# A spectral filter and an MLP on one core: a new order of loads, transposes and matmuls

## The chip, the cores and the metric

The kernel runs on one core of one Trainium2 chip. The metric is the device time of one execution in microseconds. The kernel before took 152.96 us, the median of three runs (152.87 to 153.53). The profiled execution took 152.75 us; the span from its first to its last instruction, which the profile's pages count from, is 151.0 us.

## The reference

The input x has 2048 tokens of 640 features (bf16). Each token is normalized, and the normalized xn goes two ways. One is a filter in the frequency domain over tokens and features together; the other is a two-layer MLP. Both results and the input are added.

```python
xn = _layernorm(x, axis=-1)
X  = rfft2(xn.astype(float32)) * (w_r + 1j * w_i)        # 2048 x 321 frequencies
A  = irfft2(X).astype(bfloat16)
h  = gelu(xn @ w1 + b1)                                  # 640 -> 1536, tanh form
out = x + A + (h @ w2 + b2)                              # 1536 -> 640
```

## The kernel before

**Tiles.** The 2048 tokens lie on 128 partitions, 16 to each; tile c holds token c of every partition. A tile is 128 by 640.

**Normalization.** For each tile VectorE takes statistics in two halves (`bn_stats`, L584), joins them (L588), adds epsilon (L596), GpSimd takes the power -1/2 for two tiles at a time (L597), and VectorE normalizes (L617). The result, xn, goes two ways.

**MLP.** The first layer needs xn with the features on the partitions, `xnT`. A tile is transposed either by TensorE (five transposes into PSUM at L635, then copied out by VectorE or ScalarE) or by a DMA transpose that SyncE issues (L624); the list `BYDMA` says which tiles go by DMA. The first layer then runs over six blocks of tiles (`BLOCKS`: one, one, two, four, four, four tiles, so matmuls of 128, 256 and 512 columns) and over twelve slices `fc` of 128 of W1's 1536 columns; each slice of a block is five matmuls into one PSUM bank, which ScalarE turns into `gT` by gelu with the bias b1 (L688). W1 is loaded in three parts by `W1P`: slices 0 to 2 on ScalarE's queue, slices 3 to 6 and 7 to 11 on SyncE's. The second layer takes `gT` against W2 (four loads) and accumulates a tile's 640 outputs in two banks (`second`).

**Filter.** The Fourier transforms are matmuls with constant tables. Pairs of tiles are folded on VectorE (L650 and L654, into `xf`), multiplied by table G into `XV` (PSUM tile `aps`, eight of them), transformed along the features with table E (`bps`, groups b0 to b5 given by `GROUPS`), then along the short token axis with table M (`cps`, blocks c00 to c31 in the trace's name mtab), multiplied by the filter W on VectorE (L756, L760), and sent back by table N (`dps`, d00 to d31, ntab). These come out as `U`, are transposed by DMA (L781), go through table GE (`eps`, getab), are unfolded on VectorE (L806, L811), and the last table, H, adds them to the second layer's sums in PSUM (`fin`). VectorE adds x + b2, prepared at L834 (L865), and SyncE stores the tile. For tiles in `KEEP` the second layer's sum is made early and moved out of PSUM (L856), and the H product is added later. The filter's weights w_r and w_i come in 34 loads (`load_w`), all of which the first product at L756 waits for.

**What sets the order.** All instructions are first recorded as operations with estimated durations, priorities and dependences. A planner (`Sched.schedule`) then walks time forward and fixes one order for each engine: among what can start now it takes the highest priority. `PRIO` and `DELTA` shift priorities by kind and by buffer name, `HOLD` tells how long TensorE should look for work of the same tile shape before it changes shape, `CHAIN` fixes the order of the blocks b, c and d on TensorE, `ZONE` says in which of the eight PSUM banks each kind may stand, and late times (`WLATE` for filter weights, `W2LATE`, `HLATE`) hold a load back in the plan. A late time acts in the plan only: on the chip a queue issues its next load as soon as the waits of that load allow. SyncE's loads and transposes form one list, issued one after another; a transpose whose tile isn't normalized yet holds what stands behind it. TensorE begins with idle matmuls on zeros (`idle`, `WARM`), which stand before the first tile's transposes and between them and the first layer.

Of the kernel before, what the change touches and what calls it, by code (L numbers as in the profile page):

```python
# [13 lines left out]
D = 640  # L14
# [4 lines left out]
NFC = 12  # L19
# [68 lines left out]
HOLD = 0.08  # L88
DELTA = {'w1_1': -129.7, 'hps3_0': -215.2, 'hps5_11': -20.4, 'xe4': -26.5, 'hps3_1': -406.2, 'hps5_10': -17.0, 'hps3_3': -30.1, 'fps0_0': -223.7, 'fps7_0': -5.0, 'gT3_9': -7.7, 'hps2_11': -58.5, 'hps0_8': -390.4, 'w2_3': -67.4, 've': 53.7, 'xo4': -78.8, 'xf2': 1.3, 'gT2_8': -76.4, 'xo1': -127.1, 'cps0_1': -49.2, 'bps3': 15.1, 'e': -84.2, 'w2_1': -191.5, 'xnT14': -64.0, 'fps10_0': 12.5, 'xo2': 243.3, 'xnT15': 63.3, 'T7': 4.7, 'hps0_4': -4.8, 'st': -0.2, 'xnT6': -28.6, 'hps3_5': 72.7, 'T5': 6.2, 'hps0_0': -3.4, 'xnT5': 123.1, 'hps2_3': 3.6, 'hps2_2': -1.6, 'fps15_320': -4.3, 'yf4': 155.4, 'xf5': -104.0, 'gT5_1': -418.7, 'hps0_9': -56.7, 'xe5': 3.3, 'hps3_8': 5.3, 'U4': 12.0, 'fps6_0': 15.4, 'dps3_1': 192.6, 'mhalf': -22.4, 'xb5': 3.0, 'xb2': 82.5, 'xa5': -49.0, 'gT5_10': 6.4, 'xn2': 44.4, 'gT4_3': -9.0, 'T1': -6.3, 'aps4': -66.2, 'hps4_4': 50.5, 'xa3': -129.6, 'v15': 32.5, 'hps2_6': 67.9, 'xz6': 13.4, 'hps4_3': -8.7, 'xo10': -7.1, 'T3': -3.8, 'fps15_0': 6.4, 'cps2_1': -0.7, 'hps1_0': -49.1, 'gT0_11': -3.3, 'hps2_4': 22.7, 'os13': -338.9, 'hps5_9': -3.2, 'bps5': 28.3, 'v11': 122.4, 'gT0_2': -677.2, 'fps4_0': 10.3, 'gT0_9': -325.4, 'gT4_11': -102.1, 'gT5_3': -117.0, 'y21': 54.8, 'w2_0': 11.4, 'x12': -26.0, 'hps5_2': -12.3, 'xo8': -10.3, 'yo5': -2.7, 'Z3': 4.8, 'U7': -4.4, 'T0': 3.1, 'hps0_2': -54.0, 'gT2_4': -47.7, 'dps0_0': -63.5, 'hps0_7': -4.6, 'Z7': 118.6, 'gT0_1': -10.6, 'hps3_2': 7.1, 'os7': 9.5, 'gT3_11': -10.1, 'hps1_9': -20.0, 'Y4': -450.7, 'xnT2': 90.2, 'gT4_4': -5.7, 'yf2': 102.2, 'dps3_0': -32.1, 'xo14': 11.6, 'xa2': -0.3, 'xo9': 2.7, 'hps1_1': 170.0, 'yo0': -59.2, 'aps0': 2.3, 'eps5': 0.9, 'hps4_11': 318.5, 'xe6': -0.6, 'eps0': 22.7, 'v5': -23.8, 'xnT13': 4.1, 'gT1_7': 42.0, 'xa6': -90.2, 'U6': -8.9, 'xo7': 5.8, 'xb0': -1.4, 'T2': -49.8, 'os11': -257.0, 'gT2_9': 3.5, 'aps7': -113.2, 'U3': 10.3, 'hps5_7': -1.6, 'yo4': -12.5, 'gT0_4': -4.4, 'fps15_480': -17.1, 'xnT8': 8.7, 'm': -24.0, 'gT5_6': -0.1, 'xo15': 26.7, 'gT3_5': 540.8, 'v1': 6.6, 'hps4_10': 60.2, 'gT1_1': -33.1, 'fps1_0': 5.7, 'y22': -24.0, 'v13': -2.1, 'kps14': -347.4, 'gT0_5': -532.0, 'gT3_4': -9.8, 'gT3_1': 11.0, 'hps1_7': -10.2, 'gT4_8': -4.3, 'U2': -7.0, 'xf4': -31.0, 'gT1_11': 290.2, 'y20': -7.8, 'os10': 30.9, 'cps2_0': -344.1, 'xb3': 4.5, 'gT5_11': 123.8, 'os14': 8.4, 'os9': 65.8, 'hps1_11': 12.0, 'xf6': -24.4, 'hps3_11': -5.3, 'n': 5.9, 'fps3_0': 460.6, 'bps1': -6.0, 'gT5_0': -18.0, 'gT2_10': 3.2, 'gT4_2': 17.5, 'y25': -40.9, 'bps0': 128.4, 'hps2_9': 28.0, 'hps1_2': -0.5, 'i': -429.4, 'gT3_10': 15.1, 'hps1_3': -7.0, 'warmps': -3.7, 'hps2_8': 20.8, 'xn7': -55.7, 'gT2_7': -25.5, 'os5': 133.8, 'xo3': 12.3, 'bps2': 124.2, 'tps3': -7.1, 'os3': -90.6, 'xz4': 303.0, 'wpad': -63.1, 'v4': -13.7, 'v3': 57.5, 'b2': -2.7, 'b1ps': 451.6, 'xnT9': 7.8, 'fps2_0': -19.4, 'gT0_10': -130.4, 'hps4_7': 11.2, 'aps1': -23.2, 'x14': -2.7, 'gT3_8': 8.6, 'gT4_1': 259.1, 'kps10': -242.3, 'dps0_1': 0.6, 'gT1_4': 26.9, 'cps3_1': -20.9, 'gT1_8': 388.6, 'Y0': 3.7, 'xa1': -9.0, 'xnT7': 15.0, 'xnT0': -4.2, 'xz14': -15.5, 'x8': -20.9, 'gT5_8': 5.6, 'xe3': -0.6, 'dps1_0': 163.0}


def mm_us(n):
    return max(n / 2400.0 + 0.0027, 0.0265)
# [286 lines left out]
GROUPS = ((0, 2), (2, 3), (5, 3), (8, 3), (11, 3), (14, 2))  # L380
BYDMA = (4, 8, 9, 10, 11, 12, 13, 14, 15)
WLATE = (14.6, 0.72)
ANY = [(0, 8)]
ZONE = {'hps': [(4, 8)], 'bps': [(0, 4), (4, 8)], 'cps': [(0, 4)], 'dps': [(0, 4)], 'eps': [(0, 4)], 'fin': [(0, 8)], 'fps': [(4, 8)], 'tps': [(0, 8)], 'aps': [(0, 8)]}
PRIO = {'hps': -118.5, 'gelu': -251.6, 'pb': 89.9, 'pc': 206.3, 'filt': 461.0, 'ipc': 165.5, 'eps': 24.1, 'fin': -47.0}
AHEAD = 1
EARLY = 4
CHAIN = "b0 b1 c01 c00 b2 c10 d00 d01 c11 b4 b3 c21 c20 d10 d11 b5 c31 d21 d20 c30 d30 d31".split()
XASPLIT = [((0, 1, 2, 3, 4),)] * 7 + [((0, 1), (2, 3, 4))]
KEEP = (2, 3, 4, 5, 7, 8, 12)  # L390
RES = 261.9
W2LATE = (31.0, 2.4)
HLATE = 59.8
WARM = (46, 6)
X2POS = 2
FLAG = 1.4
# [3 lines left out]
def bass_parallel_sum__spectral_gfnet__dense_activation_gelu__prompt_kernel(  # L400
# [21 lines left out]
    with ExitStack() as es:  # L422
# [54 lines left out]
        def load(dst, src, buf, nbytes, after=(), reads=(), rate=395e3, q="sp", late=0.0):  # L477
            return K.op([(q, 0.6 if buf is B_w else 1.0 if q == "pool" else 0.45)], 20 if q == "pool" else 400, lambda e, _: e.dma_start(dst, src), reads=reads, writes=[buf], after=after, nbytes=nbytes, rate=rate, late=late)  # L478
# [35 lines left out]
        idle(WARM[0], 5.25 - 0.1 * (55 - WARM[0]))  # L514
# [61 lines left out]
        norm_ops, ring_ops, a_ops, first_ve = [], [], [], []  # L576
        B_rs = [Buf(f"rstd{c}") for c in range(16)]
        for c0, n in [(0, 1), (1, 1)] + [(c, 2) for c in range(2, 16, 2)]:
            pr = 100 - c0 / 2
            B_mv, B_ve, B_r = Buf("mv"), Buf("ve"), Buf("r")  # L580
            for c in range(c0, c0 + n):
                B_st = Buf("st")
                for h in range(2):
                    st = K.op([("dve", 0.393)], pr, lambda e, _, c=c, h=h: e.bn_stats(stats[:, c, 6 * h:6 * h + 6], view(X, c * D + H2 * h, [[1, H2]])),  # L584
                         reads=[B_x[c]], writes=[B_st], gate=first_ve if c == 1 else [])
                if c == 1:
                    second_st = st
                K.op([("dve", 0.119)], pr, lambda e, _, c=c: e.bn_aggr(mv[:, c, :], stats[:, c, :]), reads=[B_st], writes=[B_mv])  # L588
            a, b = c0, c0 + n
            if not c0:  # L590
                o = K.op([("act", 0.2)], 300, lambda e, _: e.activation(ve[:, 0:1], mv[:, 0, 1:2], ACT.Sqrt, bias=epst[:]), reads=[B_mv, B_eps], writes=[B_ve])
                K.op([("dve", 0.09)], 110, lambda e, _: e.reciprocal(rstd[:, 0:1], ve[:, 0:1]), reads=[B_ve], writes=[B_r])
                K.op([("act", 1.45)], 300, lambda e, _: e.activation(first[:, 1:2], warm[:, 0:1], ACT.Gelu_apprx_tanh), reads=[B_warm], gate=[o])
                first_ve = [o]
            else:
                K.op([("dve", 0.09)], pr, lambda e, _, a=a, b=b: e.tensor_scalar_add(ve[:, a:b], mv[:, a:b, 1], 1e-5), reads=[B_mv], writes=[B_ve])  # L596
                K.op([("pool", 0.65)], pr, lambda e, _, a=a, b=b: e.tensor_tensor(out=rstd[:, a:b], in0=ve[:, a:b], in1=mhalf[:, a:b], op=ALU.pow),  # L597
                     reads=[B_ve, B_mh], writes=[B_r])
            for c in range(a, b):
                B_rs[c].writers += B_r.writers + B_mv.writers  # L600

        for pair in range(8):
# [10 lines left out]
            for n in range(2):  # L613
# [9 lines left out]
                if c in BYDMA:  # L623
                    K.op([("sp", 1.3)], 500, lambda e, _, c=c, n=n, xnv=xnv: e.dma_start_transpose(xnT[:, :, 128 * c:128 * c + 128], xnv(n, 0, [[1, D]])),  # L624
# [12 lines left out]
                tp = K.op([("pe", 5 * mm_us(128))], pr, xt, reads=[B_xn, xn, B_id], writes=[tps], alts=[[("128", 5 * mm_us(128))]])  # L637
                if not c:
                    pe([("128", 0.1)], 200, lambda: [(psb(B_b1ps.slot, [[1, NFC]]), b1t[:], ident[0:NFC, 0:NFC], True, True)], reads=[B_b1, B_id], writes=[B_b1ps], gate=[tp])
                    K.op([("act", 0.2)], 200, lambda e, _: e.activation(b1col[:], psb(B_b1ps.slot, [[1, NFC]]), ACT.Copy), reads=[B_b1ps], writes=[B_b1c])  # L640
                    idle(WARM[1], WARM[1] * mm_us(128), gate=[tp])
                for k, (js, engs) in enumerate(EVAC[c] if c < 2 else [((0, 5), "both")]):
                    w = 128 * (js[1] - js[0])
                    K.op([x for x in (("dve", 0.066 + w / 1860.0), ("act", act_us(w))) if engs in ("both", x[0])], pr,
                         copy(lambda c=c, js=js: xnT[:, js[0]:js[1], 128 * c:128 * c + 128],
                              lambda tpv=tpv, js=js: tpv(*js).rearrange("p (j t) -> p j t", j=js[1] - js[0])),
                         reads=[tps], writes=[B_xnT[c]] + ([B_xnTp[c][k]] if c < 2 else []))
            pr = 100 - pair - FLAG
# [75 lines left out]
        for P in range(4):  # L724
# [53 lines left out]
            for pair, U, B_u in zip(two, Us, B_us):  # L778
                for qq in range(2):
                    q = 2 * pair + qq  # L780
                    K.op([("sp", 1.3)], 500, lambda e, _, q=q, qq=qq, U=U, uv=uv: e.dma_start_transpose(  # L781
# [12 lines left out]
        for gi, (c0, n) in enumerate(GROUPS):  # L794
# [20 lines left out]
            for i in range(n):  # L815
# [18 lines left out]
                res_ops.append(K.op([("dve", 0.74)], RES - c / 10, lambda e, _, c=c, xov=xov, shaped=shaped: e.tensor_tensor(  # L834
# [67 lines left out]
```

## Time and profile before

| what | value |
|---|---|
| time, median of 3 | 152.96 us |
| span of the profiled execution | 151.0 us |
| TensorE busy | 142.7 us, 95% |
| VectorE busy | 114.2 us, 76% |
| ScalarE busy | 81.0 us, 54% |
| the filter weights' issues on SyncE | 34, from 7.2 to 52.0 us |
| W1's parts: issue to landing | 480 KB 4.3 us, 800 KB 6.6 us, 640 KB 12.0 us |
| DMA transposes of xn: to landing | 2.7 / 3.0 / 4.6 us (least, median, most) |
| last store issued | 148.97 us |

A busy TensorE isn't TensorE at its peak: matmuls overlap[...]. The starts of matmuls that stand in a row tell the pace better: ten of 128 columns take 0.56 us, seven of 512 columns 1.51 us. The engines' starts in the timelines are counted from the first instruction. "SPq" is SyncE issuing a DMA; the time shown is that of the issue, and the landing comes later. A wait is put down to what released the instruction last, and "issue" means that the profile shows no releaser.

### The profile page before, as it was taken

Reading aid. Unit: us, or ns where it says so; the run is one execution under the profiler, and the core shown is the slowest. Engines: PE = TensorE matmul, PEld = TensorE weight load, DVE = VectorE, ACT = ScalarE, POOL = GpSimd, SP = SyncE. Lnnn points to the kernel's source line nnn. Section 1 sums busy time; section 2 is a strip of 40 time slices with the busy share of each in tenths; the row PEclk is TensorE's granted clock in tenths of the full one; section 3 lists DMA queues with packets and bytes.
Section 4 is the critical chain, followed back from the end, with each engine's and each line's share of the span. In section 5 each row is a group of like instructions: output and inputs, shape, how many; then the busy total and the mean of one; then the engine's idle time right before and its main releaser. Section 6 shows DMA issues by size and latency. Waiting matters only on the chain.

```text
span 151.0 us, 4055 instructions
## 1 busy us (share of the span) xinstructions
PE 142.7 (95%) x1701; PEld 88.3 (58%) x1725; DVE 114.2 (76%) x244; ACT 81.0 (54%) x143; POOL 9.3 (6%) x22
## 2 busy tenths in 40 slices
PE   7999899999999997999998999999999999999993
PEld 7879797544556352355354455555667665655573
DVE  1899998999932579497999999942489998656433
ACT  3679989765896779678999471230124204100000
POOL 1120341124000000000000000000000000000000
DMA  4999977668898575083006406215100232202022
GB/s 128 360 400 386 218 125 156 132 130 122 220 212 172 131 207 218 4 114 64 2 4 83 95 4 122 56 21 119 40 0 6 85 130 87 87 4 107 23 87 87
DMA packets 29609, 17.93 MB, mean 119 GB/s; under 512 B 18424, under 2 KB 28280, under 8 KB 29592
## 3 DMA queue, kind: packets, MB, share of 16 engines
q1 hardware_dynamic: 28552, 16.47, 42.9%
q0 software_dynamic: 240, 0.69, 2.3%
q10 hardware_dynamic: 800, 0.52, 1.1%
q8 instruction: 13, 0.21, 0.6%
q14 instruction: 4, 0.03, 0.1%
HBM read 10.96 MB, written 2.62 MB: 90 GB/s over the span
## 4 chain that ended last, share of the span: by engine, by line
PE 75%; DMA 8%; ACT 5%; DVE 4%; SPq 4%; issue 3%
PE ps L483 75%; DMA W<-in_B_w_dram 8%; SPq L478 4%; DVE T L756 2%; ACT gT L688 1%; DVE Z L760 1%; ACT T L496 1%; ACT U L496 1%; ACT XV L496 1%; DVE Y L497 1%; DVE xnT L856 0%; ACT Y L496 0%; ACT xnT L496 0%; DVE W L865 0%
## 5 line engine op out<-in xcount | busy, mean ns | idle before, releaser
L483 PE MATMUL ps<-xnT,W 128*128 128x512 bf16 (+2 forms) x350 | 55.0, 306 | 2.1 <-issue 1.0
L483 PE MATMUL ps<-W,gT 128*128 128x512 bf16 (+3 forms) x384 | 54.5, 293 | 1.3 <-issue 0.6
L483 PEld LDWEIGHTS ps<-W,gT 128*128 128x128 bf16 x396 | 30.1, 98 | 22.6 <-issue 1.2
L483 PEld LDWEIGHTS ps<-xnT,W 128*128 128x128 bf16 x360 | 28.7, 98 | 22.1 <-issue 2.1
L688 ACT ACTIVATE gT<-ps,b1col 128x512 bf16<-128x512 f32 (+2 forms) x72 | 36.4, 554 | 6.6 <-PE ps L483 5.9
L496 ACT ACTIVATE Wf<-ps 128x960 bf16<-128x960 f32 (+1 forms) x8 | 7.0, 903 | 23.7 <-PE ps L483 23.7
L584 DVE BATCH_NORM_STATS2 stats<-X 128x6 f32<-128x320 bf16 x32 | 14.1, 470 | 2.3 <-DMA X<-in_A_x_dram 2.3
L756 DVE TENSOR_TENSOR T<-Y,Wf 128x1288 bf16<-128x1288 bf16 x16 | 12.3, 823 | 1.0 <-DMA Wf<-in_A_w_i_dram 1.0
L496 ACT ACTIVATE Xb<-ps 128x960 bf16<-128x960 f32 (+1 forms) x9 | 9.8, 1140 | 2.8 <-PE ps L483 2.6
L811 DVE TENSOR_TENSOR Wf<-Wf 128x960 bf16<-128x960 bf16 (+1 forms) x12 | 6.7, 599 | 5.7 <-PE ps L483 5.5
L496 ACT ACTIVATE XV<-ps 128x1280 bf16<-128x1280 f32 (+1 forms) x8 | 9.3, 1158 | 1.5 <-PE ps L483 1.5
L496 ACT ACTIVATE U<-ps 128x512 bf16<-128x512 f32 (+1 forms) x14 | 5.4, 448 | 8.0 <-PE ps L483 8.0
L496 ACT ACTIVATE Y<-ps 128x644 bf16<-128x644 f32 x10 | 6.9, 712 | 3.1 <-PE ps L483 3.1
L654 DVE TENSOR_TENSOR T<-T 128x512 bf16<-128x512 bf16 (+1 forms) x32 | 8.5, 317 | 0.1
L865 DVE TENSOR_TENSOR W<-ps,X 128x640 bf16<-128x640 f32 (+2 forms) x10 | 6.7, 688 | 2.2 <-PE ps L483 2.2
L865 DVE TENSOR_TENSOR W<-ps,xnT 128x640 bf16<-128x640 f32 x8 | 6.5, 819 | 1.9 <-PE ps L483 1.9
L806 DVE TENSOR_TENSOR Wf<-Wf 128x960 bf16<-128x960 bf16 (+1 forms) x12 | 6.9, 597 | 0.9 <-ACT Wf L496 0.7
L597 POOL TENSOR_TENSOR rstd<-ve,mhalf 128x2 f32<-128x2 f32 (+1 forms) x8 | 5.9, 736 | 27.0 <-DVE ve L596 27.0
L483 PE MATMUL ps<-getab,XV 32*128 32x160 bf16 (+1 forms) x128 | 7.5, 242 | 0.0
L483 PE MATMUL ps<-etab,XV 32*128 32x160 bf16 (+1 forms) x128 | 7.2, 232 | 0.3 <-ACT T L496 0.3
L497 DVE CAST Y<-ps 128x644 bf16<-128x644 f32 x6 | 5.0, 827 | 3.2 <-PE ps L483 3.2
L483 PEld LDWEIGHTS ps<-etab,XV 32*128 32x128 bf16 (+1 forms) x128 | 5.5, 95 | 3.0 <-ACT T L496 0.8
(58 smaller groups left out, 125.6 us busy)
## 6 DMA issues: line engine op xcount, KB each, us to landing
out_dram<-W SPq DMA_DIRECT2D x15, 160.0 KB, 1.8
X<-in_A_x_dram SPq DMA_DIRECT2D x7, 320.0 KB, 8.4
W<-in_B_w_dram SPq DMA_DIRECT2D x4, 480.0 KB, 4.7
Wf<-in_A_w_r_dram SPq DMA_DIRECT2D x15, 80.2 KB, 3.3
Wf<-in_A_w_i_dram SPq DMA_DIRECT2D x15, 80.2 KB, 3.2
W<-in_B_w_dram SPq DMA_DIRECT2D x1, 800.0 KB, 6.6
W<-in_B_w_dram SPq DMA_DIRECT2D x1, 640.0 KB, 12.0
gtab<-c_G SPq DMA_DIRECT2D x1, 512.0 KB, 7.4
```

The lines of the kernel that those rows point to most:

```text
L478: return K.op([(q, 0.6 if buf is B_w else 1.0 if q == "pool" else 0.45)], 20 if q == "pool" else 400, lambda e, _: e.dma_start(dst, src), ...
L483: ins = e.matmul(o_, lhsT=lw, rhs=rh, start=st, stop=sp_, skip_group_check=True)
L496: return e.activation(dst(), src(), ACT.Copy, scale=scale)
L497: return e.tensor_copy(dst(), src())
L584: st = K.op([("dve", 0.393)], pr, lambda e, _, c=c, h=h: e.bn_stats(stats[:, c, 6 * h:6 * h + 6], view(X, c * D + H2 * h, [[1, H2]])), rea ...
L597: K.op([("pool", 0.65)], pr, lambda e, _, a=a, b=b: e.tensor_tensor(out=rstd[:, a:b], in0=ve[:, a:b], in1=mhalf[:, a:b], op=ALU.pow), read ...
L654: ring_ops.append(K.op([("dve", dve_us(4 * w, 2))], pr, lambda e, _, op=op, x1v=x1v, xfv=xfv, o_=o_, o0=o0, o1=o1, w=w: e.tensor_tensor(ou ...
L688: K.op([("act", act_us(128 * nt, 1))], pr + PRIO["gelu"], lambda e, _, c0=c0, nt=nt, fc=fc, hps=hps: e.activation(gT[:, fc, 128 * c0:128 * ...
L756: filt_ops.append(K.op([("dve", dve_us(4 * KP, 2))], pr, lambda e, _, k=k, Y=Y, TB=TB, pair=pair: e.tensor_tensor(out=view(TT, TB.slot * 8 ...
L806: K.op([("dve", dve_us(320 * n, 2))], pr + 2, lambda e, _, k=k, op=op, yo=yo, y2=y2, n=n: e.tensor_tensor(out=view(Wf, Y2 + y2.slot * 3 * ...
L811: K.op([("dve", dve_us(320 * n, 2))], pr + 3, lambda e, _, k=k, op=op, y2=y2, yf=yf, n=n: e.tensor_tensor(out=view(Wf, YF + yf.slot * 3 * ...
L865: K.op([("dve", dve_us(w))], 95, lambda e, _, os_=os_, fps=fps, o0=o0, w=w, xov=xov, shaped=shaped, base=base: e.tensor_tensor(out=shaped( ...
```

## The change

The change moves loads and transposes on the queues, and has the planner make all five orders again.

- W1's middle part (slices 3 to 6, 640 KB) is issued third of the large loads on SyncE's queue, before tiles 2 and 3, instead of last. On ScalarE's queue W1's first part goes ahead of the identity table.
- Seven tiles (9 to 15) are transposed by DMA instead of nine (4 and 8 to 15); tiles 4 and 8 go through TensorE.
- 18 of the 34 filter weights are issued before the first DMA transpose, instead of three.
- The group sizes of the feature transforms are 3, 2, 3, 3, 3, 2 instead of 2, 3, 3, 3, 3, 2; `CHAIN` is another order of the same 22 blocks; `KEEP` holds eight tiles, (2, 4, 5, 7, 8, 9, 11, 14), instead of seven.
- 43 and 5 idle matmuls instead of 46 and 6. The small matmul that turns b1 stands after the first eviction of tile 0.
- The statistics of tile 2 wait in the plan for tile 1's variance, by a new gate.
- The planner's durations for issues are measured ones: 0.47 and 0.645 for loads, 1.33 for a DMA transpose, 0.82 for the residual add, where 0.45, 0.6, 1.3 and 0.74 stood.

It is meant to have W1 whole early, so that the first blocks can run without a gap, and the filter's weights landed before VectorE wants them, with a plan whose times are nearer to the chip's.

```diff
-HOLD = 0.08
+HOLD = 0.12
...
-GROUPS = ((0, 2), (2, 3), (5, 3), (8, 3), (11, 3), (14, 2))
-BYDMA = (4, 8, 9, 10, 11, 12, 13, 14, 15)
-WLATE = (14.6, 0.72)
+GROUPS = ((0, 3), (3, 2), (5, 3), (8, 3), (11, 3), (14, 2))
+BYDMA = (9, 10, 11, 12, 13, 14, 15)
+WLATE = (11.9, 0.84)
...
-EARLY = 4
-CHAIN = "b0 b1 c01 c00 b2 c10 d00 d01 c11 b4 b3 c21 c20 d10 d11 b5 c31 d21 d20 c30 d30 d31".split()
+EARLY = 3
+CHAIN = "b0 b1 c00 c01 b2 c11 d01 d00 c10 b4 b3 c20 d11 c21 d10 b5 c30 c31 d20 d21 d30 d31".split()
...
-KEEP = (2, 3, 4, 5, 7, 8, 12)
-RES = 261.9
-W2LATE = (31.0, 2.4)
-HLATE = 59.8
-WARM = (46, 6)
+KEEP = (2, 4, 5, 7, 8, 9, 11, 14)
+RES = 23.0
+W2LATE = (30.5, 0.9)
+HLATE = 50.3
+WARM = (43, 5)
 X2POS = 2
-FLAG = 1.4
+FLAG = 2.3
...
-            return K.op([(q, 0.6 if buf is B_w else 1.0 if q == "pool" else 0.45)], ...
+            return K.op([(q, 1.0 if q == "pool" else 0.645 if buf is B_w or buf in B_w2 else 0.47)], ...
...
-                         reads=[B_x[c]], writes=[B_st], gate=first_ve if c == 1 else [])
+                         reads=[B_x[c]], writes=[B_st], gate=first_ve if c == 1 else second_ve if c == 2 else [])
...
-                    K.op([("sp", 1.3)], 500, lambda e, _, c=c, n=n, xnv=xnv: e.dma_start_transpose(...
+                    K.op([("sp", 1.33)], 500, lambda e, _, c=c, n=n, xnv=xnv: e.dma_start_transpose(...
...
-                if not c:
-                    pe([("128", 0.1)], 200, ... b1t[:], ident[0:NFC, 0:NFC] ..., gate=[tp])
+                    if not c and not k:
+                        pe([("128", 0.1)], 200, ... b1t[:], ident[0:NFC, 0:NFC] ..., gate=[ev])
...
-                res_ops.append(K.op([("dve", 0.74)], RES - c / 10, ...
+                res_ops.append(K.op([("dve", 0.82)], RES - c / 10, ...
```

`DELTA` and `PRIO` have other values throughout and are left out here. W1's middle part and the 18 weights are moved by these priorities and late times; no line of the load section itself differs.

The orders that follow, as the built programs have them. SyncE, before: two X loads, b1, X, W1 last part, gtab, six X, W1 middle part, three weights, transpose of tile 4, thirteen weights, tiles 8 and 9, two weights, tiles 10 and 11, tiles 12 and 13, W2, a weight, tiles 14 and 15, W2, fifteen weights, two W2, htab. SyncE, changed: two X loads, b1, W1 middle part, X, W1 last part, gtab, six X, eighteen weights, tiles 9, 10 and 11, two W2, tile 12, W2, three weights, tile 14, thirteen weights, tile 15, W2, tile 13, htab.

TensorE up to the first block with etab, counted in matmuls of the first layer (128, 256, 512 columns): before, 15 of 128, then tile 1's transposes; changed, 20 of 128, tile 1's transposes, 66 of 128, the first `aps`. The 512-column matmuls start after tiles 2 to 7 are transposed in both. The first matmul that waits for DMA transposes of 9 to 11 is the 41st of 512 columns in the changed order.

## The prediction

> **What bounds the kernel now.** I read the page first, then the chain of waits, then the timelines of TensorE and SyncE, because the change touches loads and order and hardly any arithmetic. The page's busy times, and its slices for four resources:
>
> ```profile
> PE 142.7 (95%) x1701; PEld 88.3 (58%) x1725; DVE 114.2 (76%) x244; ACT 81.0 (54%) x143; POOL 9.3 (6%) x22
> ...
> PE   7999899999999997999998999999999999999993
> ...
> DVE  1899998999932579497999999942489998656433
> ACT  3679989765896779678999471230124204100000
> ```
>
> TensorE is busy in every slice of 3.8 us, so the end moves only if its work or its waits do. VectorE and ScalarE are full in the first ten slices (to 40 us) and again near 60 to 90 us: there they can hold TensorE. The waits, from the timeline of TensorE, the chain in order of time, and the list of waits:
>
> ```profile
> 17.69 0.72 PE L483 MATMUL ps<-gtab,T 128*128 128x128 bf16 x10
> 18.93 3.08 PE L483 MATMUL ps<-xnT,W 128*128 128x256 bf16 x38 [0.52 <-DMA W<-in_B_w_dram]
> ...
> 60.25 0.52 PE L483 MATMUL ps<-Z,ntab 32*32 32x320 bf16 x32 [0.90 <-issue]
> 80.38 0.98 PE L483 MATMUL ps<-etab,XV 128*128 128x160 bf16 x16 [0.27 <-ACT T L496]
> 97.39 1.58 PE L483 MATMUL ps<-W,gT 128*128 128x128 bf16 x11 [0.29 <-DVE xnT L856]
> ```
>
> ```profile
> 6.76 12.04 DMA W<-in_B_w_dram
> ...
> 74.90 0.71 ACT Y L496
> ...
> 79.67 0.67 ACT T L496 x2
> ```
>
> ```profile
> DVE T L756 <- DMA Wf<-in_A_w_i_dram: 1.0, 1, 1.0
> ```
>
> W1's middle third is issued at 6.76 and lands 12.04 later, at 18.80; TensorE waits 0.52 for it. The 0.90 before 60.25 is put down to "issue", but it is the first inverse matmul (ntab), which reads what VectorE's filter made, and VectorE sat 1.0 waiting for filter weights. So the last filter weight sets that time. Between 74.90 and 80.34 the chain runs on ScalarE alone, which empties PSUM more slowly than TensorE fills it; that ends in the 0.27 at 80.38. All other waits after 10 us are of 0.3 and less. SyncE's timeline shows why the weights are late:
>
> ```profile
> 16.90 1.32 SPq L624 DMA_TRANSPOSE xnT<-Z  x1
> 18.27 9.32 SPq L478 DMA_DIRECT2D Wf<-in_A_w_r_dram  x13
> 27.64 2.60 SPq L624 DMA_TRANSPOSE xnT<-Z  x2
> ...
> 42.41 9.63 SPq L478 DMA_DIRECT2D Wf<-in_A_w_i_dram  x15
> ```
>
> Its queue stands still from 10.9 to 16.9, behind a transpose whose tile isn't normalized yet, and ends its weights at 52.0.
>
> [...] the third issued last of W1 and X landed last, at 18.80. [...] Here ScalarE's first third of W1 (issued 1.14, 480 KB) took 4.3 us beside SyncE's X loads[...]. [...] This trace shows ten in 0.56 us when they stand in a row (21.85 to 22.41 to 22.97), so I take 0.056 each.
>
> **The change part by part.** I split TensorE's time into work (its listed matmuls at the measured starts: 0.056, 0.109 and 0.215 us for 128, 256 and 512 columns) and lag (start less work less the first 1.0).
>
> *Work.* Tiles 4 and 8 go back to TensorE: 10 x 0.056 = +0.56. Three warm-ups fewer at the head and one later, 0.106 each: -0.43. Sum +0.13. Their two evictions (0.48 on VectorE, 0.70 on ScalarE) lie on engines that are nearly full then; they are in the opening below. The group sizes 3,2,3,3,3,2, and ident issued after W1 on ScalarE, change no work; ident lands later, behind part of W1's 480 KB (issued 1.14, landed 5.4), while the warm-ups end at 5.55 instead of 5.87. I take nothing for the pair: what the shorter warm-up gives, ident may take.
>
> *W1's middle third, third in SyncE's queue.* 640 KB now pass ahead of x2, the last third and gtab. At the pace at which gtab's 512 KB followed the last third (9.13 to 10.42, 397 KB/us) that costs them 1.6 us; at the pace of the third itself (last X landing 16.24, its own 18.80) 2.6 us. I take 2.2: x2 at 8.4, last third at 11.3, gtab at 12.6. In the new order TensorE puts blocks 0 and 1 first and meets the last third after 43 matmuls behind tile 1's transposes, at about 8.5 + 43 x 0.056 = 10.9 (wait 0.4; between 0 and 0.8), and gtab 23 matmuls later (12.6; 0 to 0.4). So the 0.52 wait goes, and a 0.4 one comes.
>
> *The opening.* VectorE sets the rest: two statistics 0.80, aggregate 0.12, normalization 0.36, folds 0.40 and 0.25 each, copy 0.43. Following its new list: tiles 2 and 3 are normalized at 13.3 (11.9 before: x2 is later and pair 0's folds come first). From there to tile 7's normalization stand eleven statistics (4.4), two copies (0.87), two folds (0.8), aggregates and small pieces (0.75) and four normalizations (1.44): 8.3, and 0.6 waited for tile 3's transposes: 22.2. Its transposes and copy let the first 512-column matmul start at about 23.5. Before it started at 24.72. Work ahead of it is 20.8 before and 20.1 now, so the lag falls from 2.95 to 2.4: -0.55 (0 if the loads take the long end, -1.1 if the short).
>
> *Seven tiles by DMA, behind 18 weights.* The 18 issues are done by 7.2 + 3.6 + 15 x 0.64 = 20.5. Tiles 9, 10, 11 are normalized at 27.6, 28.0, 28.8, so weights hold no transpose up. Issues of 1.28 each start at 27.7, 29.0, 30.3; landing takes 2.7 to 3.0 where nothing else ran, 4.6 at most, so tile 11 lands at 33.0 to 34.9. The first matmul that reads it has 30.0 of work ahead: 1.0 + 30.0 + 2.4 = 33.4. Wait 0 to 1.5; I take 0.15, since the slow pair ran beside GpSimd's two table loads, now later. Pair 1's folds end near 29.9, where TensorE wants them at 29.8: 0.15. Sum +0.3.
>
> *The weights.* After tile 11: two W2 1.2, tile 12 1.3, W2 and three weights 2.6, tile 14 1.3, thirteen weights 8.3: last issue at about 46, landing by 50. VectorE wants them when the second forward block ends, 51.1 + 1.0 + 2.7 = 54.8. The wait goes whole: -0.9. Tile 13, now last, is issued near 48.5 and lands by 53; its block of 512 starts near 58. Hidden.
>
> *The order of the second half.* The waits of 0.27 and 0.29 belong to the old order: -0.55. The new one puts one forward block (c21) 2.1 us behind an inverse block (d11), and both use the same four PSUM banks (ZONE gives cps and dps 0 to 3); ScalarE alone must empty them, 2 x (0.61 + 0.29) with a gelu ahead: 0.3. And d30 stands 7.5 us behind c31, while two evictions of 0.7, four products (3.04), one add (0.82) and four sums (1.7) take 7.2 with VectorE's backlog of residual adds in front: 0.2. Each could be 0 to 0.6. Eight kept tiles instead of seven add one 0.82 add to VectorE after 85 us, under TensorE's products. HOLD, PRIO and DELTA cost nothing beyond this order.
>
> Sum: 0.13 - 0.55 + 0.3 - 0.9 - 0.55 + 0.5 = -1.07, and 152.96 - 1.07 = 151.9.
>
> **The rivals.** *All waits go:* opening -1.1, no late tile 11, 0.1 new: 0.13 - 1.1 - 0.9 - 0.55 + 0.1 = -2.3, 150.6. For it speaks that W1 is whole by 11.3, so two blocks are free to run early; against it that ScalarE needs 24 gelus x 0.32 = 7.6 us for them, where TensorE needs 6.7. *A wash:* opening 0, because the wait for the middle third turns into waits for the last third, gtab and ScalarE; tile 11 0.3; new waits 1.0; -0.9 - 0.55 + 0.13: 0.0, 152.9. The two full engines speak for it. *Slower:* ident and x0 share the DMA engines with W1 from the first issue (opening +0.4), tile 11 takes 4.6 (+1.5), new waits 1.1, less 0.9 and 0.55, plus 0.13: +1.7, 154.6. For it speaks that TensorE's list is fixed, so that one late tile holds everything behind it; against it that nothing else is in the queue when tile 11 goes.
>
> **How the numbers follow.** Forecast 0.46, all waits 0.14, wash 0.23, slower 0.17. The bounds of the unknown costs (opening 0.55 to both sides, tile 11 +1.35, the two banks' waits 0.6 down and up) reach from the first rival to past the wash; leaving out the slow case and a little of the best gives 150.5 to 153.6. Faster by over 0.5% means under 152.2: the first two cases, less what of the forecast is above it and plus little: 0.58. Within: 0.25. Slower: 0.17.
>
> **What would show it.** Right: the first 512-column matmul near 23.5; no wait of VectorE for Wf; W1's thirds land near 8 and 11.3; a short wait for the last third before 12; the first block with etab starts 44.0 of work in, near 47.8; the last filter weight lands by 50. Wrong: TensorE idle 1 us or more before the 41st 512-column matmul (tile 11), or tile 7's transposes after 23.5, or TensorE idle over 0.5 before c21 or d30. A first real matmul later than 7.4 would say that ident or x0 lost the race against W1.

## The result

The changed kernel took 156.54 us (median of 6, 154.60 to 159.92) where the kernel before took 152.94 (152.76 to 153.53): slower, where 151.9 was forecast. The ratio of the times is 1.0129 (95% interval 1.0091 to 1.0167); it leaves out executions more than 1.5% above the fastest of their kernel, three of the six here, so it is smaller than the medians suggest. The profiled execution took 155.54 us, its span is 153.7 us (before: 151.0).

The page after, with the lines that answer to those shown of before:

```profile
PE 144.7 (94%) x1731; PEld 87.0 (57%) x1731; DVE 114.4 (74%) x244; ACT 83.1 (54%) x146; POOL 9.4 (6%) x22
...
PE   7689969999999989899999999969999999999993
...
DVE  0788599999991447869599999957269929688852
ACT  3589856778899777787989465321025510020100
```

TensorE now has slices of 6: the second, the sixth, and the one from 100 to 104 us. Its timeline shows these waits:

```profile
5.96 0.44 PE L636 MATMUL ps<-ident,Z 128*128 128x128 bf16 x5 [1.00 <-DVE Z L618]
...
7.14 0.73 PE L483 MATMUL ps<-xnT,W 128*128 128x128 bf16 x10 [0.35 <-ACT xnT L496]
8.49 0.73 PE L483 MATMUL ps<-xnT,W 128*128 128x128 bf16 x10 [0.62 <-DMA W<-in_B_w_dram]
...
22.81 0.81 PE L636 MATMUL ps<-ident,Z 128*128 128x128 bf16 x10 [1.33 <-DVE Z L618]
...
55.49 1.25 PE L483 MATMUL ps<-xnT,W 128*128 128x512 bf16 x5 [0.52 <-DMA xnT<-Y]
...
64.58 0.52 PE L483 MATMUL ps<-Z,ntab 32*32 32x320 bf16 x32 [0.50 <-issue]
...
102.84 0.52 PE L483 MATMUL ps<-Z,ntab 32*32 32x320 bf16 x32 [1.26 <-ACT U L496]
```

The chain of what ended last, in order of time, names what lies behind three of them:

```profile
7.48 13.05 DMA X<-in_A_x_dram
...
20.82 0.70 POOL etab L478
21.55 0.73 POOL rstd L598
22.30 0.46 DVE Z L618
...
50.56 4.88 DMA xnT<-Y
...
97.37 4.63 DMA XV<-U
102.02 0.77 ACT U L496 x2
```

*Tiles 4 to 7 (22.81, transposed in the order 6, 7, 4, 5).* Two things stand side by side here. The first is VectorE's list. The new order loads X for tiles 6, 8, 10 and 12 before tiles 4 and 5, which land at 18.93 (11.25 before). VectorE waits 1.58 for them, while what the roots of tiles 6 and 7 need stands behind that in its list, and then works through its list up to 22.20 before it comes to the normalizations:

```profile
18.96 1.28 DVE L584 BATCH_NORM_STATS2 stats<-X 128x6 f32<-128x320 bf16 x3 [1.58 <-DMA X<-in_A_x_dram]
...
22.01 0.19 DVE L588 BATCH_NORM_AGGREGATE mv<-stats 128x2 f32<-128x12 f32 x1
22.30 1.67 DVE L618 TENSOR_SCALAR Z<-X,mv,rstd 128x640 bf16<-128x640 bf16 x4
```

The second is GpSimd's queue. It holds the load of etab ahead of the inverse roots (L598) of tiles 4 to 7. That load waits for the last load of X, which lands at 20.52, so the first root ends at 22.28. The chain names the root, but VectorE's list alone would have let the normalizations start only some 0.2 earlier (a_etab, below).

*Tile 12 (55.49).* The last of the seven DMA transposes is that of tile 12; tile 13's is the fourth, so the order given under "The change" has these two the wrong way round. Tile 12's is issued at 50.56, behind a load of W2, and takes 4.88; TensorE was ready for it at 54.97.

*d31 (102.84).* There are three U buffers. ScalarE's copy into U waits until the DMA transposes have read what the buffer held before (issued at 97.37, landed at 102.00), and d31 waits for that copy.

### The profile page after: what moved, and what is told of

Its sections match the earlier page's. It is cut to its first block, busy times and chain, and to the rows that moved or that the text cites. A ratio compares the mean times of both kernels' runs of the same rounds, so it can differ in the third digit from the quotient of the medians.

```text
span 153.7 us, 4097 instructions
## 1 busy us (share of the span) xinstructions
PE 144.7 (94%) x1731; PEld 87.0 (57%) x1731; DVE 114.4 (74%) x244; ACT 83.1 (54%) x146; POOL 9.4 (6%) x22
## 4 chain that ended last, share of the span: by engine, by line
PE 74%; DMA 15%; SPq 5%; issue 1%; ACT 1%; DVE 1%; POOL 1%
PE ps L483 72%; DMA X<-in_A_x_dram 8%; SPq L478 4%; DMA xnT<-Y 3%; DMA XV<-U 3%; PE ps L636 1%; ACT U L496 1%; SPq L625 1%; POOL rstd L598 0%; DVE XV L497 0%; POOL etab L478 0%; ACT gtab L496 0%; SPq L784 0%; DVE Z L618 0%; DVE W L868 0%
## 5 line engine op out<-in xcount | busy, mean ns | idle before, releaser
L483 PE MATMUL ps<-xnT,W 128*128 128x512 bf16 (+2 forms) x360 | 57.3, 308 | 1.6 <-DMA W<-in_B_w_dram 0.6
L483 PE MATMUL ps<-W,gT 128*128 128x512 bf16 (+3 forms) x396 | 56.3, 295 | 0.0
L496 ACT ACTIVATE Wf<-ps 128x960 bf16<-128x960 f32 (+1 forms) x9 | 7.6, 880 | 31.7 <-PE ps L483 31.7
L496 ACT ACTIVATE Y<-ps 128x644 bf16<-128x644 f32 x11 | 7.5, 715 | 3.2 <-PE ps L483 3.0
L598 POOL TENSOR_TENSOR rstd<-ve,mhalf 128x2 f32<-128x2 f32 (+1 forms) x8 | 6.1, 764 | 21.1 <-DVE ve L596 21.1
L809 DVE TENSOR_TENSOR Wf<-Wf 128x960 bf16<-128x960 bf16 (+1 forms) x12 | 6.8, 598 | 0.5 <-ACT Wf L496 0.2
L483 PEld LDWEIGHTS ps<-getab,XV 32*128 32x128 bf16 (+1 forms) x128 | 6.4, 146 | 1.2
L497 DVE CAST Y<-ps 128x644 bf16<-128x644 f32 x5 | 4.1, 827 | 4.0 <-PE ps L483 2.8
L763 DVE TENSOR_TENSOR Z<-T 128x644 bf16<-128x644 bf16 x16 | 7.0, 488 | 0.1
```

The lines of the kernel that those rows point to most:

```text
L483: ins = e.matmul(o_, lhsT=lw, rhs=rh, start=st, stop=sp_, skip_group_check=True)
L496: return e.activation(dst(), src(), ACT.Copy, scale=scale)
L497: return e.tensor_copy(dst(), src())
L763: K.op([("dve", dve_us(2 * KP, 2))], pr, lambda e, _, TB=TB, Z=Z, r=r, op=op: e.tensor_tensor(out=view(Zb, Z.slot * 4 * KP + r * KP, [[2 * ...
L809: K.op([("dve", dve_us(320 * n, 2))], pr + 2, lambda e, _, k=k, op=op, yo=yo, y2=y2, n=n: e.tensor_tensor(out=view(Wf, Y2 + y2.slot * 3 * ...
```

## Experiments

All edits but those that say otherwise are moves in the finished order: `put(engine, a, b)` takes operation a out of its engine's order and sets it behind b (with False: ahead of b). Waits of TensorE for which no line is shown are counted from the start of the matmul before, less the pace of such matmuls; the profile's own idle time is some 0.16 lower. Where the profile's figure is meant, the text says so.

**The waits of the trace, one by one.** Six kernels undo one cause each, two of them, or all.

```diff
 a_etab    +put("pool", e, r[3])          # etab's load behind the roots of tiles 4 to 7
 a_x4      +put("sp", x4, x6, False)      # X of tiles 4, 5 ahead of tiles 6, 7
 a_etab_x4 both
 a_t12     +put("sp", xnT12, xnT13)       # tile 12 transposed right behind tile 13
 a_u       +for U in Us: if U.slot == 2: U.slot = 3, its waits on the U before dropped
           -view(U2, off, dims)
           +view(xb3, off, dims) if U.slot == 3 else view(U2, off, dims)
 a_all     all four
```

> Changed kernel, with the load of etab moved on GpSimd's queue behind the inverse roots of tiles 4 to 7; nothing else moves. Theory (GpSimd's queue stood behind etab, which waits for the last X load, landed 20.52): the roots of tiles 6 and 7 come at about 20.8, those of 4 and 5 at about 21.7 instead of 21.5 and 22.3, and TensorE's 1.3 us wait before tile 4's transposes falls by 0.5 to 0.8; time about 154.2. Rival (the X load of tile 4, landed 18.93, is what counts): the wait stays within 0.3 of 1.3, time 154.9 as in the changed kernel.

> Changed kernel, with the X load of tiles 4 and 5 issued ahead of that of 6 and 7 instead of fifth of six; nothing else moves. Theory (etab stands ahead): VectorE's 1.6 us wait for X goes, but the roots still follow etab at 21.5, so TensorE's wait stays over 1.0; time within 0.4 of 154.9. Rival (the late X load is what counts): TensorE's wait goes, time about 153.6.

> Changed kernel with both moves: etab behind the roots of tiles 4 to 7, and X of tiles 4 and 5 first. Theory (the two waits stand side by side, and either alone hides the other): TensorE's wait of 1.3 goes whole, time about 153.4, more than the sum of the two single moves. Rival (the wait is the queue's total load): some 1 us of it comes back at the next tiles, time above 154.3.

> Changed kernel, with the last of the seven DMA transposes (landed 55.44 behind thirteen filter weights) moved to right behind the fourth; nothing else moves. Theory: TensorE's wait of 0.5 to 0.8 before the first matmul of the last block of four tiles goes, time lower by 0.6 to 0.8, about 154.2. Rival (the wait passes to the next transpose, landed 51.84, or is given back at the first inverse block, whose filter waits for the weights): no change within 0.3.

> Changed kernel, in which one of the two last U buffers (tiles 12 to 15) stands in the memory of Xb, dead by then, instead of in the third U slot, so that its eviction need not wait for two DMA transposes of the U before; nothing else moves. Theory: TensorE's wait of 1.3 to 1.4 before the last inverse block (d31) goes; since the last four transposes then start earlier too, time lower by 1.2 to 1.4, about 153.6. Rival (the block waits for PSUM or for VectorE's sums anyway): under 0.3.

> Changed kernel with all four moves: etab behind the roots, X of tiles 4 and 5 first, the seventh transpose behind the fourth, the last U in Xb's memory. Theory (three faults of order that add up, 1.3 + 0.7 + 1.3): 154.9 - 3.3 = 151.6, under the kernel before. Rival (VectorE and ScalarE, full in the opening, give part of it back): 152.5 to 153.5.

| kernel | median us (range, executions) | ratio to before |
|---|---|---|
| a_etab | 155.14 (153.86 to 156.44, 4) | 1.0108 (1.0045 to 1.0172) |
| a_x4 | 157.07 (154.29 to 157.15, 4) | none (one of four executions left) |
| a_etab_x4 | 155.01 (153.75 to 155.67, 4) | 1.0142 (1.0094 to 1.0190) |
| a_t12 | 155.58 (154.78 to 156.91, 4) | 1.0173 (1.0105 to 1.0241) |
| a_u | 154.24 (153.67 to 155.89, 4) | 1.0124 (1.0041 to 1.0207) |
| a_all | 153.21 (152.77 to 155.30, 12) | 1.0031 (1.0000 to 1.0063) |

The traces of a_etab_x4, a_t12, a_u and a_all were taken at full clock, and the waits that were aimed at are gone in them. No single repair can be told from the changed kernel by its time. Together they take its ratio from 1.0129 to 1.0031, and the span from 153.7 to 151.0. That is where the rival of a_all put it (152.5 to 153.5), not the 151.6 of its theory: part of the gain goes into waits of 0.91 for W1's middle third and of 0.59 for VectorE's copies at 15.7 (profile's figures).

For tiles 4 to 7 the pair a_etab_x4 settles the matter. GpSimd's timeline, then VectorE's:

```profile
19.92 0.69 POOL L598 TENSOR_TENSOR rstd<-ve,mhalf 128x2 f32<-128x2 f32 x1 [6.95 <-DVE ve L596]
20.85 0.77 POOL L598 TENSOR_TENSOR rstd<-ve,mhalf 128x2 f32<-128x2 f32 x1 [0.23 <-DVE ve L596]
21.48 0.70 POOL L478 DMA_DIRECT2D etab<-c_E  x1
```

```profile
21.19 1.47 DVE L618 TENSOR_SCALAR Z<-X,mv,rstd 128x640 bf16<-128x640 bf16 x4
```

The roots run as soon as VectorE has their inputs, the normalizations start at 21.19 instead of 22.30, and TensorE doesn't wait for them. How much each of the two moves gives alone isn't shown: in the traces of a_etab and a_x4 TensorE stood at half clock for 3.41 and 6.82 us in the opening (below), so TensorE was later than the tiles, and that their wait is gone proves nothing. VectorE's timeline suggests that etab alone gives little. From the statistics of tile 4 to the normalizations it takes 3.34 in the changed kernel, 3.16 in a_etab and 3.15 in a_etab_x4. But with X alone moved, the first root would still stand behind etab and end near 22.3 (an estimate from the chain above), so both moves are needed.

**Two parts of the change in the kernel before.**

```diff
 b_w1mid +put("sp", w1_1, b1t)             # W1's middle third third in SyncE's queue
 b_w23   +put("sp", xnT4, W[9])            # ten filter weights ahead of tile 4's transpose,
         +seven of the tail ahead of tile 8's
```

> Kernel before, with W1's middle third alone moved third in SyncE's queue; all other orders stay. Theory (what it passes lands 2.2 to 2.6 later, VectorE waits for X and falls behind): TensorE's 0.52 wait for the third goes, but it waits 1 to 2 us elsewhere before 25 us; time 153.5 to 154.5. Rival (the third is free there): -0.4, time 152.5.

> Kernel before, with the filter weights alone issued earlier: ten instead of three ahead of tile 4's transpose, and seven of the last fifteen moved ahead of tile 8's transpose, so that SyncE no longer stands still for 6 us; all other orders stay. Theory (the last weight, landed 54.5, set the first inverse block): last weight lands near 50, VectorE's 1.0 and TensorE's 0.9 wait go, time about 152.1. Rival (weights on the DMA engines delay tile 4 or the transposes of 8 to 11): no gain or up to 0.5 slower.

Measured: 155.94 (155.19 to 156.60), ratio 1.0198 (1.0146 to 1.0250); and 155.95 (153.39 to 158.16), ratio 1.0091 (1.0052 to 1.0130). Neither part is a gain in the old order. In b_w1mid the loads of X take longer to land (the median of seven is 9.1 us, 8.4 before), VectorE, idle from 7 to 9 us, waits for x2 in front of tile 1's normalization, and TensorE idles 3.05. In b_w23 the weights pass beside W1's middle third, which lands at 21.57 instead of 18.80; TensorE waits 3.06 for it (profile's figure). Eleven of its fifteen executions had a halved clock (below); the other four took 153.39 to 154.41. The last weight landed at 53.26, VectorE no longer waits for one, and yet it stands still before its first product:

```profile
58.53 2.31 DVE L756 TENSOR_TENSOR T<-Y,Wf 128x1288 bf16<-128x1288 bf16 x3 [0.85 <-ACT gT L688]
```

TensorE's wait before its first inverse block is 0.78 where it was 0.90 (profile's figures). So the weights' arrival was not all of it.

**What the weights' wait was.** VectorE's first product with the weights waits on 34 semaphores, one for each load. In the trace after, all weights had landed nearly 7 us before, and VectorE still stood 0.85 in front of it. Two kernels give all 34 loads one semaphore:

```diff
-                    o.sem, o.count = nc.alloc_semaphore(f"d_{o.seq}"), 16
+                    (o.name == "W": one semaphore for all, count 16 * 34; waited on once)
```

> The kernel before with one semaphore for all 34 loads of filter weights instead of one each, so VectorE waits once instead of 34 times ahead of the first product with the weights. Theory A (the 0.97 us before that product are 34 wait instructions of about 25 ns; it is 0.84 where the weights had long landed): the gap of VectorE falls to 0.1 to 0.3, TensorE's 0.90 before its first inverse matmul falls to 0.1 to 0.3, and the time falls by 0.6 to 0.8: ratio 0.995. Theory B (VectorE waits for the last weight, as the prediction had it): gap and time unchanged, ratio 1.000.

> The changed kernel with one semaphore for its 34 loads of filter weights. Theory A (the weights land in time in the changed kernel, and what is left of VectorE's gap of 0.85 ahead of the first product are 34 wait instructions): the gap goes, TensorE's 0.67 before d01 goes, 0.5 to 0.7 us less than the changed kernel in the trace. Theory B (the gap is ScalarE's copy): the gap stays.

VectorE's timeline after:

```profile
57.28 0.83 DVE L497 CAST Y<-ps 128x644 bf16<-128x644 f32 x1 [0.93 <-PE ps L483]
58.95 2.31 DVE L759 TENSOR_TENSOR T<-Y,Wf 128x1288 bf16<-128x1288 bf16 x3 [0.85 <-DVE Y L497]
```

and in a_onesem:

```profile
57.44 0.83 DVE L503 CAST Y<-ps 128x644 bf16<-128x644 f32 x1 [0.93 <-PE ps L489]
58.30 2.31 DVE L765 TENSOR_TENSOR T<-Y,Wf 128x1288 bf16<-128x1288 bf16 x3
```

The gap is gone, and so is TensorE's 0.50 before d01. So here 34 waits on semaphores that were long up took 0.85: 25 ns each. The ratio is 1.0076 (1.0052 to 1.0100) against 1.0129 (1.0091 to 1.0167); the intervals overlap, so the gain rests on the trace. In b_onesem (152.87, ratio 0.9991, 0.9967 to 1.0015) the gap stays, 1.09, put down to the last weight's load, which lands at 55.05. In the kernel before, VectorE was free at 53.65 and the last weight landed at 54.54, 0.89 later, while the 34 waits take 0.85. So both theories hold there: two costs of nearly the same length lay on each other, and removing one leaves the other.

**Why the executions scatter.** The granted clock, as a mean over the span, was 0.99 or less in 4 of 6 executions of the changed kernel and in 2 of 43 of the kernel before (its largest group of executions). One stretch of 3.41 us at half clock makes 0.989. The stretches view of b_w1mid (us from the start; then the length, each engine's busy time, the granted clock, the DMA share and GB/s) shows how:

```profile
7.39:10.81 3.42, 0.54 (x10) 0.37 (x8) 1.74 (x6) 0.89 (x3) 0.00 (x0) 1.00 1.07 385
10.81:14.22 3.41, 3.39 (x31) 3.02 (x32) 3.41 (x14) 1.96 (x5) 0.86 (x1) 0.50 1.03 396
14.22:17.63 3.41, 3.41 (x58) 3.34 (x56) 2.53 (x8) 3.06 (x8) 0.00 (x0) 1.00 0.87 275
```

Behind a stretch of 3.42 us in which TensorE was busy for 0.54, it has 3.41 us at half clock, with 31 matmuls where the next 3.41 us have 58. As an estimate, half of 3.41, that is 1.7 us of work lost. Two kernels fill idle stretches with empty matmuls, to tell whether the idleness is the cause:

```diff
 a_fill     +4 at the head, 6 ahead of block 0, 14 ahead of its first use of W1's middle third
 b_mid_fill b_w1mid, +48 ahead of tile 1's transposes
```

> The changed kernel with 24 empty matmuls more on TensorE in the opening: 4 behind the 43 warm-ups at the head, 6 ahead of the first matmul of block 0, 14 ahead of the first matmul that reads W1's middle third. All lie in stretches where TensorE idles (1.0 before tile 0's transposes, 0.35 and 0.6 to 2.1 after), so they should cost 0 to 0.3 us. Theory A ([...]): no execution shows a granted clock of 0.99 or less, while the changed kernel had it in 4 of 6; median 154.6 to 155.6 instead of 156.5. Theory B (the spread comes from loads that land at different times, the clock follows something else): still half of the executions at 0.99 or less, median near 156.5.

> The kernel before with W1's middle third third in SyncE's queue, as tried before (155.94, and a halved clock in 4 of 4 executions), and 48 empty matmuls in the 3.05 us in which TensorE waited there for tile 1. The wait is the same, only TensorE is busy in it. Theory A (idleness halves the clock for the next 3.41 us): no execution at a clock of 0.99 or less, and 1.2 to 1.7 us less: 154.2 to 154.8. Theory B (the clock falls for another reason, the loads or the start of the kernel): clock and time as without the empty matmuls.

The same stretches in b_mid_fill:

```profile
7.39:10.81 3.42, 3.19 (x58) 3.01 (x54) 1.42 (x4) 0.92 (x3) 0.00 (x0) 1.00 1.06 380
10.81:14.22 3.41, 3.02 (x48) 2.68 (x49) 3.41 (x14) 2.48 (x8) 0.86 (x1) 1.00 1.04 395
```

No execution of six had the halved clock, where all four of b_w1mid had it, with the same loads and the same wait: here it was the idleness. The time did not fall with it (155.80, 155.39 to 156.89), against the theory's 154.2 to 154.8: what TensorE gained it gave back at 37.1, waiting 1.36 instead of 0.26 for a tile that comes by DMA transpose. a_fill is inconclusive: 155.81 (154.61 to 158.42), two of six at 0.989. In its trace the middle third came at 9.39, later than the filling reached, and the wait ahead of tiles 6 and 7 was 1.9. How a halved stretch goes with the time is best seen in a_onesem, with 22 executions: median 154.5 at full clock (12), 156.9 at 0.988 to 0.989 (8). That is 2.4 apart, where by the estimate the clock itself takes 1.7; the rest isn't traced.

**A version that beats both.** all_t1s has the four repairs, one semaphore, ident ahead of W1 on ScalarE, tile 1's transposes ahead of the matmuls that wait for the middle third, and 14 empty matmuls. all_v adds one move. a_id has the ident move alone; b_w1x8s is the kernel before with one semaphore and the middle third two loads of X earlier.

```diff
 all_t1s +put("act", ident, w1_0, False); put("pe", tps1, hps0_4, False)
         +put("act", xnT1, gT0_4, False)
 all_v   +put("dve", xnT2 and xnT3, xn1[1])   # copies ahead of the next statistics
```

> The changed kernel with the four repairs tried before (etab's load behind the roots, X of tiles 4 and 5 first, tile 12 transposed early, a U buffer of its own), and four more: ident first in ScalarE's queue, tile 1's transposes ahead of the matmuls that read W1's middle third, 14 empty matmuls in TensorE's idle stretches ahead of them, one semaphore for the filter weights. Repairs alone left 153.2. If the idle stretches and the waits add up as the traces say (0.66 before d01, 0.4 of the opening, 1.7 for a halved clock in one execution of four): 151.6 to 152.4, and no execution at a clock of 0.99 or less. If the middle third itself sets the opening, the 1.07 stays and only the 0.66 goes: 152.5.

> The changed kernel with all eight repairs and one more: VectorE copies the transposes of tiles 2 and 3 out of PSUM before, and not after, the first statistics of the next load of X. In the version without it VectorE sat 1.54 us for that load while TensorE waited 1.19 for the copies. If that wait is real and not only passed on: it goes, 0.8 to 1.2 us less, 151.4 to 152.0, ratio 0.992 or lower, faster than both kernels. If the load of X sets the opening anyway (the statistics of the following tiles): no change, 152.8.

> The changed kernel with one edit: ident is issued ahead of W1's first part on ScalarE's queue, as in the kernel before. The prediction took nothing for this pair. Theory A (W1's 480 KB ahead of ident and beside x0 delay both): x0 lands near 3.2 instead of 3.71, tile 0's transposes start near 5.4 instead of 5.96, and the middle third lands up to 0.4 sooner: 0.3 to 0.5 us. Theory B: the idle time of TensorE only moves behind the first ten matmuls, where the middle third holds it: no change of the time, 155 to 156.5.

> The kernel before with one semaphore for the filter weights, and W1's middle third two places earlier in SyncE's queue, ahead of the last two loads of X. If the third's place is what cost TensorE 0.52 at 18.9, that wait goes too (the third lands near 16.3) and the last X lands near 18.8, where VectorE doesn't yet want it: 151.6 to 152.0, ratio 0.992. If moving it only passes the wait on to X, as the early place did in the changed kernel: 152.2 to 153.0, with VectorE waiting for X near 18.

all_t1s: 152.78 (152.02 to 154.01, 14), ratio 0.9997 (0.9970 to 1.0024), above the 151.6 to 152.4 forecast; no halved clock. VectorE stood there 1.54 for a load of X, with the copies that TensorE wanted behind it. all_v: **151.99 (151.66 to 152.06, 6), ratio 0.9914 (0.9892 to 0.9936)**, as forecast, and 0.9% faster than the kernel before. Its TensorE timeline has the middle third and tiles 4 to 7 without a wait:

```profile
8.27 0.44 PE L642 MATMUL ps<-ident,Z 128*128 128x128 bf16 x5
8.55 4.41 PE L489 MATMUL ps<-xnT,W 128*128 128x128 bf16 x76
...
21.05 0.79 PE L642 MATMUL ps<-ident,Z 128*128 128x128 bf16 x10
```

a_id: 155.46, ratio 1.0124 (1.0080 to 1.0169). x0 landed 0.5 earlier, tile 0's transposes began at 5.56 instead of 5.96, and tile 6's at 22.70 instead of 22.81: the gain ended in that wait. So there was no change, as its theory B has it, though the middle third wasn't what held it. b_w1x8s: 152.98, ratio 0.9995 (0.9965 to 1.0026): the wait at 18.9 went, and TensorE waited 1.47 ahead of tile 1's transposes (9.04) and 0.92 for a DMA transpose (36.17) instead.

## Why the prediction was wrong

- **The opening, -0.55: the step that failed most.** By the prediction's own reckoning the lag at the first matmul of 512 columns is 25.22 - 20.1 - 1.0 = 4.1 after and 2.9 before: +1.2. The loads were sized well (last third 11.54 for 11.3, gtab 12.83 for 12.6; x2 0.9 late, 9.31 for 8.4, so that tiles 2 and 3 were normalized at 13.85, not 13.3), but the step said "VectorE sets the rest" and put VectorE's waits for X at nothing. It took the order of X's loads as unchanged, and so missed the 1.58 that VectorE waits for tile 4; nor did it follow GpSimd's queue, where etab held the roots beside it. Tile 7 was normalized at 23.1 where 22.2 was forecast, and tiles 4 and 5, which the prediction thought done by then, came behind it (transposes at 23.68). The middle third costs 0.62, where a wait for the last third was expected and none came. Nothing for ident and x0 was wrong by 0.5 in its place (x0 landed at 3.71 instead of 3.23, and TensorE idled 1.00 ahead of tile 0's transposes, which the fewer idle matmuls were to bring forward) and right in the end, as a_id shows.
- **The weights, -0.9: half of the mechanism.** The last weight landed at 51.33 (50 was forecast) and VectorE waits for none. But TensorE's wait only fell from 0.90 to 0.50: -0.4. "So the last filter weight sets that time" was half true: the 34 semaphore waits lay under it and took its place.
- **The last transpose, "hidden": failed.** It is tile 12's, not 13's. It was issued at 50.56, not 48.5, and landed at 55.44, not 53; TensorE was ready for its block at 55.0, not 58: +0.52.
- **The order of the second half.** The waits of 0.27 and 0.29 went, as said. The new ones did not come where they were put (c21, d30) but at d31, 1.26 for the 0.5 forecast: DMA transposes still reading a U buffer, and the prediction never looked at these buffers. (The times that the prediction lists before d30 add up to 7.0, not 7.2, and its 7.2 + 3.6 + 15 x 0.64 is 20.4, not 20.5; neither matters.)
- **Tile 11, +0.3: right or less.** It landed at 34.48, within 33.0 to 34.9, and nothing waited.
- **Work, +0.13: close.** One of the four idle matmuls left out stood behind tile 0's transposes, where they start 0.056 apart, not 0.106.
- **Not foreseen: the halved clock**, in four of six executions. It isn't in the profiled one, so it is no part of the sum below, but it is in the median.

Sum for the profiled execution, at full clock: 0.13 + 1.2 - 0.4 + 0.52 - 0.56 + 1.26 = 2.15 of the 2.7 us by which the span grew; the rest lies in small gaps that were not followed. The rival that forecast 154.6 was nearer in size by luck: tile 11 was not late, ident and x0 cost nothing in the end, and the new waits stood elsewhere. Open stays why executions with one halved stretch reach 158 to 160, which 1.7 us don't explain, and why the middle third lands between 8.4 and 9.7 from one trace of the changed order to the next.

## What to carry to other kernels

When an order is made anew, follow each queue to its end, those that are hardly busy too. Here a load of X that had moved down its queue held VectorE, and a load on GpSimd held a root of 0.7 us beside it; by the traces either alone would have held TensorE. When a wait is to go, ask what else ends at the same time, such as the wait instructions themselves or the engine that feeds the other operand. Repairs of waits in series show their worth only together, so judge them by the trace one by one and by the time as a whole.

## What the runs showed of the hardware

- *The halved clock.* In b_w1mid, b_w23 and a_etab TensorE has one stretch of 3.41 us at half clock (from 10.81, 21.30 and 8.75), in a_x4 one of 6.82 (from 8.90). In the 3.41 or 3.42 us just ahead TensorE was busy for 0.54, 0.76, 1.84 and, in a_x4, 1.76 us. In a_u, 3.42 us with 2.02 busy (from 5.01) were followed by full clock. In a_x4's half clock TensorE was busy for 2.60 of the first 3.41 us and for all of the second; in b_w23's it was busy for 3.00 and in a_etab's for 3.21, and both were back at full clock after one such stretch. What decides between half and full isn't shown, nor why some executions of a kernel have such a stretch (four of six of the changed one) and others none.
- *Waits.* A wait on a semaphore that was already up took VectorE 25 ns (0.85 for 34, gone in a_onesem). The 34 are a visible gap, and the profile puts it down to something else: VectorE's own copy in the changed kernel, ScalarE's gelu in b_w23.
- *DMA transposes.* In the changed kernel's trace 14 of 23 took 2.6 to 2.7 us to land, and nine took 3.1 to 6.6. The slowest two, 6.55 and 6.20, cost nothing; those of 4.88 and 4.63 ended up on the chain. Tile 12's, 4.88, landed 0.74 after the load of W2 (480 KB) that was issued 0.6 before it.
